# Turned blocks of a tile taken in the first two segments of the next tile, weight pieces in the others, and Q and K stored by one transfer

## The chip, the cores and the metric

The kernel runs on one core of one Trainium2 chip. The metric is the time of one execution on the device, in microseconds (us). One core has no second, slower state of a die to look out for: every run used here counts as fast, so all are compared with each other. "Ratio" always means the mean time of one kernel's fast runs over the mean of the other's fast runs of the same rounds, with a 95% interval, so it is not quite the ratio of the medians that stand beside it.

## The reference, cut to what matters

The reference computes the forward pass and all gradients of one layer: attention that runs over 64 segments in turn, each handing 8 memory rows to the next, then a gated feed-forward block. This is the recurrence that the change touches:

```python
mem = mem0                                    # 8 rows of 448
for s in range(n_seg):                        # 64 segments of 32 rows
    xs = x[:, s * seg_len:(s + 1) * seg_len, :]
    h = jnp.concatenate([mem, xs], axis=1)    # 40 rows
    q = jnp.einsum('btd,dhe->bhte', h, Wq)    # 16 heads of 256
    k = jnp.einsum('btd,dhe->bhte', h, Wk)
    v = jnp.einsum('btd,dhe->bhte', h, Wv)
    scores = jnp.einsum('bhqe,bhke->bhqk', q, k) * scale
    ...
    p = _softmax(scores, axis=-1)
    o = jnp.einsum('bhqk,bhke->bhqe', p, v)
    o = jnp.einsum('bhte,hed->btd', o, Wo)
    mem = o[:, :M, :]                         # the next segment waits for this
    outs.append(o[:, M:, :])
```

A segment cannot start before the previous one has given its memory rows, so the 64 segments are one chain. The backward pass needs Q, K, P and V of every segment, the attention output X_o with tokens on the partitions, and the weights turned. The kernel stores or turns all of these while the chain runs.

## The kernel before

The text of the kernel is the order in which work is emitted. A scheduler then places each instruction in its engine's list, by priority (the chain has the highest) and by when its own model expects the data to be ready. What is not tied to the chain can be moved far ahead of its place in the text. Each engine then works through its list.

Turning is done by DMA transposes that SP (SyncE) issues. They land in one of two staging buffers, and POOL (GpSimd) issues the save from there to DRAM:

```python
def stg():                      # the two staging buffers, dealt in turn
    rot[0] += 1
    for fn in unsaved.pop(rot[0] % 2, ()):
        fn()
    return stg_b[rot[0] % 2]

def save(*pairs):
    def fn():
        for out, in_ in pairs:
            nc.gpsimd.dma_start(out=out, in_=in_)              # L503
    unsaved[rot[0] % 2] = [fn]

def to_token_major(blk, t, ins=None):      # one tile (4 segments): two halves
    for hf in range(2):
        ot = stg()
        with tc.issue_after(ins) if ins is not None else nullcontext():
            nc.sync.dma_start_transpose(out=ot.rearrange(...), in_=blk[:, 16*hf:16*hf+16, :]...)   # L543
        save((dr["X_o"][t][:, hf * 2048:(hf + 1) * 2048], ot))

def piece():                               # one piece of a weight
    ...
    T, ot = dr["T" + nm], stg()
    ... nc.sync.dma_start_transpose(out=o3, in_=Ws[:, i0:i0 + n])          # L562, L563, L568
    save(...)
```

In the loop over segments (s is the segment, t the tile, r = s % 4, jm = s % 16), the attention of one segment, cut to its order:

```python
qk_rows(s, 0); qk_rows(s, 1)               # Q, K rows: L521, L525
qk_turned(s, 0)                            # turned on PE: L535
for w, nm in enumerate("qk"):              # L689: two stores, issued by ACT
    nc.scalar.dma_start(out=dr["T1" + nm][s], in_=qk_st[:, w]...)
value_rows(0)                              # V rows, K = 128: L633
pS0 = scores(0); softmax(0, pS0)           # mask L603, scores L609, Exp on ACT L618
qk_turned(s, 1); value_rows(1)
value_rest(0)                              # V rows, last 64 of K: four matmuls, L641;
                                           # both evacuations on ACT
pS1 = scores(1); p_in = softmax(1, pS1)
value_rows(2); transposed_p(0)             # P turned on PE: L652
value_rows(3); value_rest(2, p_in)
values(0); transposed_p(1); out_proj(0, 8) # L665, L678
values(1); out_proj(8, MC)
...
```

The end of a segment, where the staging buffers are dealt:

```python
nc.gpsimd.tensor_copy(out=mh[...], in_=hT_roll[...])       # POOL copies that the chain waits for
nc.gpsimd.tensor_copy(out=mblk[...], in_=orr)
...
if r == 1:
    ot = stg(); nc.sync.dma_start_transpose(...R_b...)     # T0
    save((dr["T0" + "qk"[w]][bm], ot))
if r < 3 and s >= 4:
    piece()
...
if r == 3:
    to_token_major(xblk, t, at)                            # both halves of this tile's block
if jm == 15:
    to_token_major(mblk, NT + s // 16, at)                 # the memory rows' block, then mh
    ...
```

POOL also copies the next segment's rest rows (L465, `rest_rows`), and fetches the rows of the residual back (L585).

Of the kernel before, what the change touches and what calls it, by code (L numbers as in the profile page):

```python
# [15 lines left out]
P = 128  # L16
# [129 lines left out]
def run_all(k: _K):  # L146
    nc, tc, ctx = k.nc, k.tc, k.ctx
    S, D, M, H, Dh, HD, F = k.S, k.D, k.M, k.H, k.Dh, k.HD, k.F
    SEG, L, NSEG, NT, KC, DP, MC, DC, FC = k.SEG, k.L, k.NSEG, k.NT, k.KC, k.DP, k.MC, k.DC, k.FC
# [54 lines left out]
    def dt(name, shape, dtype=BF16):  # L204
        return dram.tile(shape, dtype, name=name)
# [3 lines left out]
    dr = dict(XN=dt("XN", [NB * P, DP]), Hh=dt("Hh", [S, D]), HN=dt("HN", [S, D]), DH=dt("DH", [S, D], FP32),  # L209
              DHb=dt("DHb", [NB * P, DP]), Zt=dt("Zt", [S, F]), DGP=dt("DGP", [S, F]), DU=dt("DU", [S, F]),  # L210
              VG=dt("VG", [NSEG, 2 * L, W2]), XR=dt("XR", [NT * 32, DP]), P_all=dt("P_all", [NSEG, P, 8 * L]),
              X_o=dt("X_o", [NB, P, MC * P]), HC=dt("HC", [NB * P, DP]), Oh=dt("Oh", [S, D]))
# [2 lines left out]
        dr["M_" + nm] = dt("M_" + nm, [NT, P, MC * 32])  # L215
    for nm in ("q", "k", "v"):
        dr["T" + nm] = dt("T" + nm, [P, MC, D])
    for nm in ("q", "k"):
        dr["T1" + nm] = dt("T1" + nm, [NSEG, P, 1024])
        dr["T0" + nm] = dt("T0" + nm, [NSEG // 8, P, W2])  # L220
    dr["To"] = dt("To", [P, KC, HD])
    dr["Td"] = dt("Td", [P, KC, F])
# [14 lines left out]
def cj(j):  # L237
    return (j % 2) * 16 + j // 2
# [111 lines left out]
def forward_chain(k: _K):  # L350
    nc, tc = k.nc, k.tc
    S, D, M, H, Dh, HD = k.S, k.D, k.M, k.H, k.Dh, k.HD
    SEG, L, NSEG, NT, KC, DP, MC, DC = k.SEG, k.L, k.NSEG, k.NT, k.KC, k.DP, k.MC, k.DC
    X2 = k.aps["A_x"][0]
    MEM0 = k.aps["A_mem0"][0]
    ident, dr, sel, maskb = k.ident, k.dr, k.sel, k.maskb
# [11 lines left out]
    qk_st = A(15, 2, 2, 512)  # L368
# [3 lines left out]
    xblk_b = [A(52 - 24 * i, 32, P) for i in range(2)]  # L372
    mblk = A(44, 32, P)
# [108 lines left out]
    def prep_tile(t):  # L482
        if t >= NT:
            return
        nc.sync.dma_start_transpose(out=hx, in_=dr["XN"][t * P:(t + 1) * P, :])
        s0 = (4 * t) % NWIN
        for kc in range(KC):
            nc.gpsimd.tensor_copy(out=hT_roll[:, kc, s0:s0 + 4, 0:SEG], in_=hx[:, kc, :].rearrange("p (g j) -> p g j", g=4))
# [5 lines left out]
    def stg():  # L494
# [11 lines that stand above are left out]
    def save_all():  # L506
        for i in (1, 2):
            for fn in unsaved.pop((rot[0] + i) % 2, ()):
                fn()
# [21 lines left out]
    def qk_turned(s, b):  # L531
        pt = k.ps1()[:].bitcast(BF16)
        for w in range(2):
            for i in range(4):
                nc.tensor.transpose(pt[:, w * 512 + i * P:w * 512 + (i + 1) * P], qk_st[:, w, b, i * P:(i + 1) * P], ident[:, :])  # L535
        for w, dst in ((0, qT_b[s % 2]), (1, kT_b[s % 2])):
            k.evac(dst[:, 16 * b:16 * b + 16, M:L], pt[:, w * 512:(w + 1) * 512].rearrange("p (c n) -> p c n", n=32), "vs"[w])

    def to_token_major(blk, t, ins=None):
        for hf in range(2):  # L540
            ot = stg()
            with tc.issue_after(ins) if ins is not None else nullcontext():
                nc.sync.dma_start_transpose(out=ot.rearrange("p (a b) -> p a b", b=P),  # L543
                                            in_=blk[:, 16 * hf:16 * hf + 16, :].rearrange("p c n -> p (c n)"))
            save((dr["X_o"][t][:, hf * 2048:(hf + 1) * 2048], ot))

    pieces = []
    for nm, Ws in (("d", k.aps["B_w_down"]), ("o", k.Wo2)):
# [6 lines left out]
    def piece():  # L555
        if not pieces:
            return
        nm, Ws, i0, n = pieces.pop(0)
        T, ot = dr["T" + nm], stg()
        if nm in "do":  # L560
            o4 = ot.rearrange("p (c n) -> p c n", c=KC)
            nc.sync.dma_start_transpose(out=o4[:, 0:3, 0:n], in_=Ws[i0:i0 + n, 0:3 * P])  # L562
            nc.sync.dma_start_transpose(out=o4[:, 3, 0:n], in_=Ws[i0:i0 + n, D - P:D])  # L563
            save((T[:, 0:3, i0:i0 + n], o4[:, 0:3, 0:n]), (T[0:64, 3, i0:i0 + n], o4[64:P, 3, 0:n]))
        else:
            m = n // P
            o3 = ot[:, 0:m * D].rearrange("p (c d) -> p c d", d=D)
            nc.sync.dma_start_transpose(out=o3, in_=Ws[:, i0:i0 + n])  # L568
            save((T[:, i0 // P:i0 // P + m, :], o3))
# [18 lines left out]
    for s in range(NSEG):  # L588
        t, r = divmod(s, 4)
        jm = s % 16  # L590
# [3 lines left out]
        xblk, om2 = xblk_b[t % 2], om_b[s % 2]  # L594
        end = s == NSEG - 1
        if due and jm % 3 == 1:
            fetch(due[0], h_t, x2_t)
        with k.prio.crit():
# [29 lines left out]
            def value_rows(b):  # L628
                pV[b] = k.ps1()
                for kc in range(KC - 1):  # L630
                    for g in range(2):
                        n = 4 * g + b
                        nc.tensor.matmul(pV[b][64 * g:64 * g + 64, 0:512], lhsT=hT_flat[:, kc, sl * L:sl * L + 64],  # L633
                                         rhs=Wv_sb[:, kc, n * 512:(n + 1) * 512],
                                         start=(kc == 0), stop=False, skip_group_check=True)
# [49 lines left out]
                k.fl.at(0)  # L685
                k.fl.at(1)
            qk_turned(s, 0)
            for w, nm in enumerate("qk"):
                nc.scalar.dma_start(out=dr["T1" + nm][s], in_=qk_st[:, w].rearrange("p b n -> p (b n)"))  # L689
            value_rows(0)  # L690
            pS0 = scores(0)
            softmax(0, pS0)
# [23 lines left out]
            else:  # L716
# [3 lines left out]
                for e in range(2):  # L720
                    nc.tensor.transpose(pm[64 * e:64 * e + 64, 96:P], om2[32:64, P:P + 64], ident[32:64, 32:64])
                to_v = nc.vector.tensor_copy(  # L722
                    out=hT_roll[:, :, (s + 1) % NWIN, SEG:L].rearrange("p (d c) m -> p d c m", d=2),
                    in_=pm[:, 0:P].rearrange("p (c d m) -> p d c m", c=2, d=2)[:, :, :, 24:32])
# [15 lines left out]
        if due and jm % 3 == 0 and jm > 0:  # L740
            n = due.pop(0)
            residual(n, h_t, x2_t, to_v)
        save_all()
        if (r == 0 and t > 0) or s == 2:
            prep_tile(t + 2)
        if r == 1:
            w = bu // 4
            ot = stg()
            nc.sync.dma_start_transpose(out=ot.rearrange("p (a b) -> p a b", b=P), in_=R_b[bm % 2][w].rearrange("p c n -> p (c n)"))
            save((dr["T0" + "qk"[w]][bm], ot))  # L750
        if r < 3 and s >= 4:
            piece()
        at = None
        if jm == 15:
            px = k.fx1()
# [4 lines left out]
            due = list(range(t - 3, t + 1))  # L760
            if end:
                at = k.fl.at(3).ins
        if r == 3:
            to_token_major(xblk, t, at)
        if jm == 15:
            to_token_major(mblk, NT + s // 16, at)
            mrow = stg()
            nc.sync.dma_start_transpose(out=mrow[:, 0:DP].rearrange("p (a b) -> p a b", b=P),
                                        in_=mh.rearrange("p c n -> p (c n)"))
            r0 = (NT + s // 16) * P  # L770
            save((dr["XN"][r0:r0 + P, :], mrow[:, 0:DP]))
    save_all()
    assert not pieces and due == list(range(NT - 4, NT))
    late = [(B(0, D), B(0.875, D)), (W(61.5, D), W(62.375, D))]
# [178 lines left out]
def backward_chain(k: _K):  # L953
    nc, tc = k.nc, k.tc
    S, D, M, H, Dh, HD = k.S, k.D, k.M, k.H, k.Dh, k.HD
    SEG, L, NSEG, NT, KC, DP, MC, DC = k.SEG, k.L, k.NSEG, k.NT, k.KC, k.DP, k.MC, k.DC
    ident, dr, sel = k.ident, k.dr, k.sel
# [6 lines left out]
    WkT_sb, Q_sb = W(32, MC, D), W(60, 16, P)  # L964
    WvT_sb, K_sb = W(64, MC, D), W(92, 16, P)
# [23 lines left out]
    def load_v(s):  # L989
        return nc.sync.dma_start_transpose(out=vT, in_=dr["VG"][s])  # L990

    def load_seg(s):
        if s < NSEG - 1:
            load_v(s)
        for nm, T_sb in (("q", Q_sb), ("k", K_sb)):
            t1 = dr["T1" + nm][s].rearrange("(g x i) n -> g i x n", g=2, x=2)
            t0 = dr["T0" + nm][s // 8].rearrange("(x s i) (g n) -> s g i x n", x=2, s=8, g=2)
            for g in range(2):
                for src, i0, i1 in ((t1[g], M, L), (t0[s % 8, g], 0, M)):
                    nc.sync.dma_start(out=T_sb[64 * g + i0:64 * g + i1].rearrange("p (x c) n -> p x (c n)", x=2), in_=src)  # L1000
        P_sb = Pb[s % 2]
        nc.gpsimd.dma_start(out=P_sb.rearrange("p h n -> p (h n)"), in_=dr["P_all"][s])
        for g in range(2):
            pool_op = nc.gpsimd.tensor_copy(out=P_bd[64 * g:64 * g + L, :, g, :], in_=P_sb[64 * g:64 * g + L, :, :])
        stores("mid", s, pool_op.ins)
# [6 lines left out]
    def stores(place, seg, ins):  # L1012

        for fn in pending.pop((place, seg), []):
            with tc.issue_after(ins):
                fn()
# [34 lines left out]
    for s in range(NSEG - 1, -1, -1):  # L1051
        t, r = divmod(s, 4)
        jm = s % 16
# [3 lines left out]
        blk = {nm: blk_b[(3 * tb + i) % 5] for i, nm in enumerate("vkq")}  # L1057
# [3 lines left out]
        if s < NSEG - 1:  # L1061
            load_seg(s)

        with k.prio.crit():
            pss = [k.ps1() for _ in range(4)]
            for j in range(MC):
                c = cj(j)
                b, jj = divmod(j, 8)
# [96 lines left out]
        if r == 0:  # L1165
# [34 lines left out]
            t1 = k.f32("f3", D, "t1")  # L1200
# [224 lines left out]
```

## Time and profile before

| reading of before | value | where it is read |
|---|---|---|
| time, median of 3 | 3183.05 us (3175.76 to 3190.79) | the times |
| profiled run | 3198.43 us, span 3196.7 us | the page |
| PE busy | 2924.5 us, 91% | the page, part 1 |
| forward chain: start of segment 0 to start of segment 63 | 14.4 to 1057.6 us | timeline of PE, first matmul of L521 of each segment |
| steady segment | 15.09 us (14.75 in segments 56 to 62) | same |
| segments 17, 18, 20, 36, 52 | 21.2, 21.3, 22.3, 22.9, 21.6 us | same |

All segment durations below are read like that, from the first matmul of L521 in one segment to the first in the next.

Most of the span is a full PE, but a few segments last 6 to 7 us longer than their neighbours. The chain of waits, followed back from the end of the program, shows why. Its lines are: start, duration, what. This is before, in segment 36 (starts at 630.5 us):

```profile
626.94 0.08 PE po L678
627.02 6.96 DMA arA<-arA
...
634.54 0.54 POOL X_o L503
635.08 5.07 DMA arB<-Oh
...
640.60 0.63 DVE stats L580
```

PE leaves the chain at 627.02 us. A turned block (arA<-arA) takes 6.96 us to land; only then can POOL issue its save. The fetch of the residual's rows (arB<-Oh) stands behind the save in POOL's list and takes another 5.07 us; then DVE has work again, and its softmax comes behind that in its own list. None of this is arithmetic of the chain: the chain waits because POOL and DVE take their lists in order.

A second kind of stall is in segment 18 (338.3 to 359.6 us). This is the same view of before, there:

```profile
339.25 6.97 DMA arA<-in_A_Wo_dram
...
346.30 0.34 ACTq L689
346.69 0.59 ACT arA L76
```

ACT stands before the first of its two issues of L689 (K's store) until a turned weight piece of SP has landed: in the program the two share a semaphore. The evacuation that the chain needs comes only after it.

### The profile page before, as it was taken

The numbers are of one execution on the slowest core, as the hardware profiler recorded it, in microseconds if no ns is written. First come the engines' busy times: TensorE is split into PE (matmuls) and PEld (weight loads), VectorE is DVE, ScalarE is ACT, GpSimd is POOL, SyncE is SP. The second block draws the span as 40 slices with busy tenths as digits, with TensorE's granted clock in tenths as the row PEclk, the third lists the DMA queues.
The fourth block names the chain that finished last, engine by engine and source line by source line (L and its number), as shares of the span: only waits on it lengthen the run. The fifth ranks groups of instructions, "written<-read, shape, count | busy, mean of one in ns | idle before, by whom it ended". The sixth has DMA issues, their size and how long they took to land.

```text
span 3196.7 us, 107765 instructions
## 1 busy us (share of the span) xinstructions
PE 2924.5 (91%) x47442; PEld 1776.2 (56%) x47442; DVE 1364.9 (43%) x3433; ACT 1057.8 (33%) x2501; POOL 723.7 (23%) x1648
## 2 busy tenths in 40 slices
PE   6899899989988869977999999999999699999998
PEld 3455455555544547645666666666666454444444
DVE  4455455455455567753444544445444201111110
ACT  2444344344434323322333333333433101110210
POOL 2232332223232221121112211112211111111111
PEclk9999999999999979988999999999999899999999
DMA  6968765867667888894454555445545898959952
GB/s 237 198 152 177 181 163 141 194 162 183 167 155 192 246 207 195 191 274 147 132 138 137 132 149 134 140 132 140 144 134 141 266 269 226 198 181 195 191 147 72
DMA packets 757305, 556.21 MB, mean 174 GB/s; under 512 B 627732, under 2 KB 656388, under 8 KB 754404
## 3 DMA queue, kind: packets, MB, share of 16 engines
q1 hardware_dynamic: 671828, 294.81, 44.2%
q0 software_dynamic: 66576, 220.95, 20.3%
q10 hardware_dynamic: 18432, 33.56, 3.1%
q8 instruction: 372, 6.09, 0.8%
q14 instruction: 97, 0.79, 0.1%
HBM read 167.32 MB, written 234.23 MB: 126 GB/s over the span
## 4 chain that ended last, share of the span: by engine, by line
PE 69%; DMA 10%; DVE 9%; issue 7%; ACT 3%; SPq 2%; POOL 1%; ACTq 0%; POOLq 0%; DVEq 0%
PE psf L1286 8%; PE po L1120 7%; PE psf L1071 7%; PE psf L633 5%; PE psf L521 4%; PE psf L1048 4%; PE psf L1307 4%; PE po L678 3%; PE fx L1184 3%; PE psf L847 2%; DVE arA L75 2%; PE fx L454 2%; PE fx L937 2%; PE fx L1291 2%; PE psf L1142 2%
## 5 line engine op out<-in xcount | busy, mean ns | idle before, releaser
L75 DVE CAST arA<-psf 128x256 bf16<-128x256 f32 (+4 forms) x997 | 470.8, 492 | 920.1 <-PE psf L1286 258.9
L76 ACT CAST arA<-psf 128x384 bf16<-128x384 f32 (+6 forms) x979 | 390.0, 420 | 1179.8 <-PE psf L1286 256.5
L1120 PE MATMUL po<-arW,arA 128*32 128x448 bf16 x6144 | 348.9, 357 | 22.8 <-DVE arA L75 20.5
L633 PE MATMUL psf<-arW,arA 128*64 128x512 bf16 x1536 | 253.3, 393 | 0.0
L1286 PE MATMUL psf<-arW,arA 128*128 128x512 bf16 x1000 | 252.0, 379 | 0.0
L1071 PEld LDWEIGHTS <-arW 128*128 128x128 bf16 x8192 | 214.1, 96 | 27.5 <-issue 27.5
L1120 PEld LDWEIGHTS <-arA 128*32 128x32 bf16 x6144 | 152.1, 97 | 135.9 <-DVE arA L75 21.7
L1286 PEld LDWEIGHTS <-arA 128*128 128x128 bf16 x1440 | 136.0, 98 | 164.8 <-issue 13.8
L1071 PE MATMUL psf<-arA,arW 128*128 128x40 bf16 x8192 | 217.7, 180 | 8.4 <-DVE arA L1146 5.1
L521 PE MATMUL psf<-arW,arA 128*32 128x512 bf16 x3072 | 193.9, 385 | 12.5 <-DVE arA L722 12.5
L847 PE MATMUL psf<-arW 128*128 128x256 bf16 x1344 | 159.3, 281 | 45.1 <-DMA arW<-arW 34.3
L847 PEld LDWEIGHTS <-arW 128*128 128x128 bf16 x1344 | 134.9, 101 | 71.5 <-DMA arW<-arW 29.1
L678 PE MATMUL po<-arW,arA 128*32 128x256 bf16 (+1 forms) x4096 | 142.4, 265 | 9.8 <-DVE arA L75 6.8
L1048 PEld LDWEIGHTS <-arW 128*128 128x128 bf16 x2048 | 87.6, 100 | 89.6 <-issue 62.9
L1048 PE MATMUL psf<-arB,arW 128*128 128x80 bf16 x2048 | 98.1, 202 | 41.4 <-DMA arW<-T0k 22.6
L454 PE MATMUL fx<-arA,arW 128*128 128x64 bf16 (+1 forms) x2048 | 84.8, 196 | 43.2 <-ACT arB L76 30.7
L1081 ACT COPY arA<-psf 128x1024 bf16<-128x1024 bf16 x128 | 123.3, 1015 | 2.3 <-PE psf L1080 0.4
L521 PEld LDWEIGHTS <-arA 128*32 128x32 bf16 x3072 | 70.5, 96 | 90.1 <-DVE arA L722 18.1
L76 ACT COPY arA<-psf 128x512 bf16<-128x512 bf16 (+2 forms) x136 | 79.0, 582 | 111.5 <-DVE arA L75 87.9
L678 PEld LDWEIGHTS <-arA 128*32 128x32 bf16 x4096 | 94.6, 97 | 30.2 <-DVE arA L75 10.2
L633 PEld LDWEIGHTS <-arA 128*64 128x64 bf16 x1536 | 85.0, 111 | 44.1 <-issue 1.4
L454 PEld LDWEIGHTS <-arW 128*128 128x128 bf16 (+1 forms) x2048 | 71.2, 99 | 65.4 <-issue 43.8
(285 smaller groups left out, 4618.6 us busy)
## 6 DMA issues: line engine op xcount, KB each, us to landing
X_o<-arA POOLq DMA_DIRECT2D x40, 512.0 KB, 4.1
T1k<-arA ACTq DMA_DIRECT2D x64, 256.0 KB
T1q<-arA ACTq DMA_DIRECT2D x64, 256.0 KB
arW<-T1q SPq DMA_DIRECT2D x128, 128.0 KB
arW<-T1k SPq DMA_DIRECT2D x128, 128.0 KB
X_v<-arA POOLq DMA_DIRECT2D x32, 512.0 KB, 5.3
X_k<-arA POOLq DMA_DIRECT2D x32, 512.0 KB, 3.8
X_q<-arA POOLq DMA_DIRECT2D x32, 512.0 KB, 3.6
```

What stands on the lines that cost most here:

```text
L75: return nc.vector.tensor_copy(out=out, in_=in_)
L76: return nc.scalar.copy(out=out, in_=in_)
L454: nc.tensor.matmul(banks[w][:, i * 64:(i + 1) * 64], lhsT=lhsT, rhs=xr[lo:hi, kc, :], start=(kc == 0 and i == 0), stop=(kc == KC - 1), ski ...
L521: nc.tensor.matmul(banks[w][32 * q:32 * q + 32, :], lhsT=hT_roll[:, kc, sl, M:L], rhs=(Wq_sb, Wk_sb)[w][:, kc, col(q, b)], start=(kc == 0) ...
L633: nc.tensor.matmul(pV[b][64 * g:64 * g + 64, 0:512], lhsT=hT_flat[:, kc, sl * L:sl * L + 64], rhs=Wv_sb[:, kc, n * 512:(n + 1) * 512], sta ...
L678: nc.tensor.matmul(pO[32 * q:32 * q + 32, 0:w], lhsT=xblk[:, j, r * SEG:(r + 1) * SEG], rhs=Wo_sb[:, cj(j), 256 * dh:256 * dh + w], start= ...
L847: nc.tensor.matmul(ps[:, f2 * 256:(f2 + 1) * 256], lhsT=Wt[:, kc, c * P:(c + 1) * P], rhs=xT[:, kc, :], start=(kc == 0), stop=(kc == KC - 1))
L1048: nc.tensor.matmul(ps[b][:, i * 2 * L:(i + 1) * 2 * L], lhsT=lhs[:, at, :], rhs=rhs_bd[:, cl // 2, :, :].rearrange("p g n -> p (g n)"), st ...
L1071: nc.tensor.matmul(pss[b][:, jj * L:(jj + 1) * L], lhsT=WoT_sb[:, kc, c * P:(c + 1) * P], rhs=do_roll[:, kc, sl, :], start=(kc == 0), stop ...
L1120: nc.tensor.matmul(pH[32 * (j % 4):32 * (j % 4) + 32, 0:D], lhsT=blk[nm][:, j, r * SEG:(r + 1) * SEG], rhs=WT[:, cj(j), :], start=(nm == " ...
L1286: nc.tensor.matmul(pa[2 * kc + g][:, 0:w], lhsT=lhs_of(b)[:, kc * P:(kc + 1) * P], rhs=rhs_of(b, g), start=(b == 0), stop=(b == nblk - 1), ...
L1307: nc.tensor.matmul(pa[i][:, 0:D], lhsT=lhs_of(b, i), rhs=rhs_of(b), start=(bi == 0), stop=(bi == len(nblk) - 1))
```

## The change

The intent is threefold. Turned blocks wait for their tile, so put them into the first two segments of the next tile, one half each; then no segment has two of them, and behind a sixteenth segment (jm = 15) three turnings stand in place of five. Weight pieces wait for nothing, so let them fill the other places. And store Q and K by one transfer of 512 KB in place of two of 256 KB, which saves ACT one issue per segment. The title of the change also says "behind the first exponential"; the text puts the store ahead of the first value rows, and leaves its place on ACT to the scheduler.

```diff
+    dr["T1"] = dt("T1", [NSEG, P, 2, 1024])
     for nm in ("q", "k"):
-        dr["T1" + nm] = dt("T1" + nm, [NSEG, P, 1024])
...
-    def to_token_major(blk, t, ins=None):
-        for hf in range(2):
-            ot = stg()
...
+    def to_token_major(blk, t, hf, ins=None):
+        ot = stg()
...
             qk_turned(s, 0)
-            for w, nm in enumerate("qk"):
-                nc.scalar.dma_start(out=dr["T1" + nm][s], in_=qk_st[:, w].rearrange("p b n -> p (b n)"))
+            nc.scalar.dma_start(out=dr["T1"][s], in_=qk_st.rearrange("p w b n -> p w (b n)"))
...
-        if r == 1:
+        if s >= 4 and ((r > 0 and jm < 15) or (jm == 0)):
+            piece()
+        if r == 2:
             w = bu // 4
             ot = stg()
             nc.sync.dma_start_transpose(out=..., in_=R_b[bm % 2][w]...)
             save((dr["T0" + "qk"[w]][bm], ot))
-        if r < 3 and s >= 4:
-            piece()
...
-        if r == 3:
-            to_token_major(xblk, t, at)
         if jm == 15:
-            to_token_major(mblk, NT + s // 16, at)
+            for hf in range(2):
+                to_token_major(mblk, NT + s // 16, hf, at)
...
+        if t > 0 and r < 2:
+            to_token_major(xblk_b[(t - 1) % 2], t - 1, r)
+        if end:
+            for hf in range(2):
+                to_token_major(xblk, t, hf, at)
...
-        for nm, T_sb in (("q", Q_sb), ("k", K_sb)):
-            t1 = dr["T1" + nm][s].rearrange(...)
+        for w, (nm, T_sb) in enumerate((("q", Q_sb), ("k", K_sb))):
+            t1 = dr["T1"][s, :, w].rearrange(...)
```

In the order in which a tile takes the two staging buffers A and B (H is half a turned block, p a weight piece), before is `p T0 p p H H`, and after is `H p H p T0 p`. As the buffers alternate, before puts pieces into both buffers, so that a piece waits for the block ahead of it in its buffer. After puts pieces into one buffer alone; only behind a sixteenth segment do three other turnings (two halves of the memory rows' block, then mh) take from both.

More of the change, by code (lines that the diff above doesn't have):

```diff
@@ L537, in qk_turned @@
             k.evac(dst[:, 16 * b:16 * b + 16, M:L], pt[:, w * 512:(w + 1) * 512].rearrange("p (c n) -> p c n", n=32), "vs"[w])
-    def to_token_major(blk, t, ins=None):
-        for hf in range(2):
-            ot = stg()
-            with tc.issue_after(ins) if ins is not None else nullcontext():
-                nc.sync.dma_start_transpose(out=ot.rearrange("p (a b) -> p a b", b=P),
-                                            in_=blk[:, 16 * hf:16 * hf + 16, :].rearrange("p c n -> p (c n)"))
-            save((dr["X_o"][t][:, hf * 2048:(hf + 1) * 2048], ot))
+    def to_token_major(blk, t, hf, ins=None):
+        ot = stg()
+        with tc.issue_after(ins) if ins is not None else nullcontext():
+            nc.sync.dma_start_transpose(out=ot.rearrange("p (a b) -> p a b", b=P),
+                                        in_=blk[:, 16 * hf:16 * hf + 16, :].rearrange("p c n -> p (c n)"))
+        save((dr["X_o"][t][:, hf * 2048:(hf + 1) * 2048], ot))
     pieces = []
@@ L994, in load_seg @@
             load_v(s)
-        for nm, T_sb in (("q", Q_sb), ("k", K_sb)):
-            t1 = dr["T1" + nm][s].rearrange("(g x i) n -> g i x n", g=2, x=2)
+        for w, (nm, T_sb) in enumerate((("q", Q_sb), ("k", K_sb))):
+            t1 = dr["T1"][s, :, w].rearrange("(g x i) n -> g i x n", g=2, x=2)
             t0 = dr["T0" + nm][s // 8].rearrange("(x s i) (g n) -> s g i x n", x=2, s=8, g=2)
```

## The prediction

> **What bounds it.** The change touches the forward chain (64 segments, 14 to 1076 us); backward reads the same bytes of Q and K. In the timeline of PE a steady segment takes 15.09 us, PE nearly full. Above that, stalls stand in a few segments (starts of L521): segments 4 and 5 about 9 us, 16 to 20 about 17, 32 to 36 about 9, 48 to 52 about 8: some 43 us. The chain of waits shows their cause: turning transfer on SP (L543, L562, L568), its save on POOL (L503), the next turning that needs the staging buffer; behind them POOL's copies and row fetches, and an ACT store (L689) that waits until an SP transfer on its semaphore has landed.
>
> **Intent.** Three turnings behind a sixteenth segment in place of five, and one ACT issue (0.33 us) fewer per segment. If every stall went, the gain were 43 us, 1.3%: over 2% faster is nearly impossible.
>
> **What moves instead** (order listings of both kernels):
> 1. Two staging buffers are taken in turn. After the change two are taken in most segments, so one gets weight pieces only, the other turned blocks and T0. The piece buffer then depends on nothing in the chain, and the scheduler hoists pieces: on SP eight stand at segments 3 to 6, twelve each at about 15 to 20, 31 to 36, 47 to 52, none between. Before, blocks that waited for their segment held them to three per four segments.
> 2. Their saves are hoisted into POOL's queue too, among the copies that the chain needs (L465 rest rows, the first 8 rows, the residual's fetches). POOL takes instructions in order (the Trainium skill, TensorE: Matmul & The Clock Gate, Part 2, says that PE alone reorders; the trace agrees: from 300 us on POOL idles 110 us at L503 for turned blocks). A piece takes about 6.5 us from issue to landing, its save 4.4: a buffer turns round in 11 us, twelve need 130 us where five to six segments give 75 to 90. POOL stands still, then DVE (it may not overwrite rows that POOL has not copied), then PE.
> 3. PE's order changes: scores of the first four heads move behind the second value rows; ACT does two evacuations (0.53 us each) before the first Exp, and both Exps follow together. P transposes and values come later.
>
> **Costing.** I laid both listed orders out with the trace's durations and landing medians (an estimate). Before comes out at 15.21 us a steady segment, with stalls in the right segments, though 30 us too little in sum. After: steady 15.46 (+0.25, some 15 us in all, on the critical path), about 30 us at segments 6 to 8 and 25 to 35 us at each of the three groups, longest at segments 19, 35 and 51 (35 to 40 us each). In sum +127 us; with landings 15% shorter +69, 25% shorter +36, 15% longer +180. I take +125. The five turnings before the feed-forward phase are reordered: within 5 us.
>
> **Predicted:** 3308 us, 3230 to 3395. Faster by over 2%: 0.03; within 2%: 0.13; slower: 0.84.
>
> **What would show it.** Segments 19, 35, 51 over 25 us, steady ones 15.3 to 15.5. POOL idle before L503 for weight pieces at least three times that of before; DVE waiting for POOL; no L567 on SP in segments 24 to 30 and 38 to 46; ACT idle longer before the first Exp. Time after the forward chain unchanged within 10 us.
>
> **What would make it wrong.** Landings much shorter when transfers run one at a time (then +30). POOL's copies having more slack than I gave them. If the burst costs nothing, 3160 to 3200 us.

## More of the kernel before

Segments 16 to 18, 32 to 34 and 48 to 50 carry extra PE work (16.45 us without a stall).

The costliest line of POOL's idle time in front of its saves, by what ended it (us, times), from before's instructions of L503 between 60 and 1070 us:

```profile
  DMA arA<-arA: 121.3, 35
```

## The result, and the profile after

| | before | after |
|---|---|---|
| time, median of 4 | 3186.92 us (3175.76 to 3193.65) | 3282.67 us (3265.64 to 3288.62) |
| ratio of fast runs | 1 | 1.0295 (1.0244 to 1.0347) |
| profiled run: time, span | 3198.43, 3196.7 us | 3265.64, 3263.8 us |
| PE busy between segments 0 and 63 (after 75 us) | 894 us | 938 us |
| start of segment 63 | 1057.6 us | 1129.2 us |
| from there to the end | 2139.0 us | 2134.7 us |
| steady segment; 56 to 62; 16 | 15.09; 14.75; 16.45 us | 15.45; 15.45; 18.05 us |
| longest segments | 36: 22.9, 20: 22.3, 5: 21.8 us | 19: 36.5, 35: 32.4, 51: 27.1, 8: 25.5 us |

The result is correct and 3% slower, and the whole loss of the profiled runs lies in the forward chain: start of segment 63 is 71.6 us later, and what follows is 4.3 us shorter. These two executions differ by 67.2 us and the medians by 95.8: before's profiled execution is slower than any of its four timed ones, after's is the fastest of its four. The account by segments below is of this pair; where the other executions lose the remaining 29 us, no trace shows.

The chain of waits of after in segment 19 (370.2 to 406.7 us), lines as above:

```profile
387.46 4.02 DMA arA<-in_B_w_gate_dram
...
392.02 2.75 DMA Tg<-arA
394.80 4.08 DMA arA<-in_B_w_gate_dram
...
399.41 2.78 DMA Tg<-arA
402.20 3.23 DMA arA<-in_B_w_gate_dram
...
405.97 0.55 POOL Tg L503
406.52 2.42 DMA arB<-Oh
```

From 379.35 us on (one more round stands ahead of these lines), the chain of the whole program runs through one staging buffer for 27 us: a weight piece is turned into it, then saved, and then the next is turned. A round takes 7.3 to 8.1 us (379.35 to 387.46 to 394.80 to 402.20). On SP, pieces from segment 16 on stand only in bursts, and each burst begins behind the turning of mh (L765) of a sixteenth segment: the scheduler did not move pieces ahead of that. At the end, as in before, POOL gets past its save and issues the fetch, and DVE follows.

What the chain does not show is why the attention waits for weight pieces that only the backward pass uses. PE stops twice in this segment, and the timelines show two paths (start, duration, engine, line, operation, out<-in, count, idle before and what ended it). The timeline of POOL, for the same segment of after:

```profile
383.84 0.57 POOL L503 DMA_DIRECT2D Tg<-arA  x1 [5.52 <-DMA arA<-in_B_w_gate_dram]
392.02 0.55 POOL L503 DMA_DIRECT2D Tg<-arA  x1 [7.62 <-DMA arA<-in_B_w_gate_dram]
392.57 0.99 POOL L465 COPY arA<-arW 128x128 bf16<-128x128 bf16 x4
...
399.41 0.54 POOL L503 DMA_DIRECT2D Tg<-arA  x1 [5.35 <-DMA arA<-in_B_w_gate_dram]
399.95 0.75 POOL L737 COPY arA<-arB 128x256 bf16<-128x256 bf16 x2
```

POOL stands idle for 7.62 us in front of one save, and the copies of the rest rows (L465) that the next segment's scores read are next in its list. Behind the save after that stand the copies of L737, and on these hangs the second stop of PE (timelines of DVE and PE):

```profile
400.39 0.23 DVE L75 CAST arB<-psf 128x64 bf16<-128x64 f32 x1 [9.34 <-POOL arA L737]
400.96 0.69 PE L664 MATMUL psf<-arB,arW 128*128 128x80 bf16 x8 [9.24 <-ACT arB L76]
```

DVE and ACT may not write new rows of `orr` before POOL has copied the old ones. The first stop does not end in POOL's list (timelines of ACT and PE):

```profile
383.39 0.33 ACTq L687 DMA_DIRECT2D T<-arA  x1
383.76 1.07 ACT L76 COPY arA<-psf 128x512 bf16<-128x512 bf16 x2 [9.28 <-DMA arA<-in_B_w_gate_dram]
384.49 0.46 PE L608 MATMUL psf<-arA 128*40 128x40 bf16 x16 [7.65 <-ACT arA L76]
```

Here ACT waits at the issue of its store until a weight piece has landed that uses the same semaphore, as in before's segment 18, and the evacuation of the turned K and Q is behind it. Of PE's stops of over 0.8 us in segments 6 to 54, 37 us end in a copy of POOL (segments 8, 19, 35 and 51, the last two with 15.09 and 9.36 us) and 19 us in ACT's store behind a turning (segments 6, 7, 8, 19, 21 and 37).

The Trainium skill, "DMA: Bandwidth & Descriptors", section "Issuing engines are not separate DMA queues", says that issuing from several engines saves only the sequencer's time, usually small beside the transfer. No run here tests that for bandwidth. Here the price is another: an issue that waits on another engine's transfer also stops everything behind it on its own engine.

The same line for L503 in after, between 60 and 1140 us:

```profile
  DMA arA<-arA: 194.4, 39
```

Turned blocks made POOL idle for 121.3 us before, and for 194.4 us now. Summed over the lines for weight pieces (in_A and in_B sources) it went from 158 to 177 us only, in 29 waits before and 39 after: no longer ones (5.5 us in the mean before, 4.5 after), but bunched in the bursts.

A long stall costs a little more than its wait. The view of stretches gives, for after's segments 19 and 41, duration and PE busy first, and the granted clock in the third number from the end:

```profile
370.20:406.70 36.50, 18.96 (x286) 10.67 (x285) 8.32 (x25) 7.24 (x18) 9.23 (x22) 0.67 0.60 158
762.65:778.10 15.45, 14.65 (x278) 8.27 (x278) 7.94 (x25) 6.79 (x17) 4.89 (x13) 1.00 0.61 180
```

and for before's segments 19 and 40:

```profile
359.50:375.50 16.00, 15.96 (x288) 8.96 (x284) 7.94 (x23) 6.56 (x16) 3.71 (x12) 1.00 0.36 82
698.72:713.81 15.09, 14.03 (x279) 7.96 (x279) 7.90 (x24) 6.76 (x17) 2.77 (x9) 1.00 1.09 217
```

In segment 19 about as many matmuls took 18.96 us of PE in place of 15.96, at a mean clock of 0.67. (one_store, below, which has after's lists and no stall here, needs 14.65 us of PE for its segment 19.) The Trainium skill, "TensorE: Matmul & The Clock Gate", Part 1, "What's actually happening", says that PE falls to half its clock after an idle window of about 3.4 us and needs as long a busy one to recover. The clock in this trace agrees with the half and with the length of the window: it is 0.50 from 378.99 to 389.23 us and from 392.64 to 406.30 us, three and four times 3.41 us. It does not agree with a whole idle window: the clock fell 2.15 and 0.91 us after PE had stopped. In the steady segments both kernels have the full clock, so the 15.45 against 15.09 us is not the clock's.

It is the lists'. PE in before's segment 40, cut to scores (L609), groups of four value matmuls (L641), turned P (L652) and values (L665):

```profile
704.16 0.54 PE L609 MATMUL psf<-arA 128*40 128x40 bf16 x14
...
705.29 0.41 PE L641 MATMUL psf<-arW,arA 64*64 64x512 bf16 x4
...
706.91 0.27 PE L652 MATMUL fx<-ident,arB 128*40 128x40 bf16 x8
...
707.78 0.41 PE L641 MATMUL psf<-arW,arA 64*64 64x512 bf16 x4
708.12 0.46 PE L665 MATMUL psf<-arB,arA 128*128 128x80 bf16 x8
```

and in after's segment 41 (lines moved by one; it starts at 762.65 us, before's at 698.72):

```profile
768.87 0.40 PE L640 MATMUL psf<-arW,arA 64*64 64x512 bf16 x2
769.20 0.38 PE L608 MATMUL psf<-arA 128*40 128x40 bf16 x16
769.50 0.40 PE L640 MATMUL psf<-arW,arA 64*64 64x512 bf16 x2
...
771.62 0.41 PE L640 MATMUL psf<-arW,arA 64*64 64x512 bf16 x3
772.31 0.27 PE L651 MATMUL fx<-ident,arB 128*40 128x40 bf16 x8 [0.27 <-DVE arB L622]
772.51 0.40 PE L640 MATMUL psf<-arW,arA 64*64 64x512 bf16 x1
...
773.17 0.46 PE L664 MATMUL psf<-arB,arW 128*128 128x80 bf16 x8
```

The scores come 5.4 us after the segment's start in before, 6.6 us in after; the first values 9.4 and 10.5 us. And four value matmuls take 0.41 us together but 0.40 us for two and 0.40 us for one: they fill the four quarters of the array at once. (The Trainium skill, "TensorE: Matmul & The Clock Gate", Part 3, "Measured speedup vs the span model", gives a group of matmuls on different tiles of the array the time of one and about 4 ns for each further one; 0.41 us for four and 0.40 for one agree.) So each split group costs a pass: PE busy is 14.65 in place of 14.03 us.

ACT in these two segments, before:

```profile
705.52 0.34 ACT L618 ACTIVATE S_sb<-S_sb 128x160 f32<-128x160 f32 x1 [0.21 <-DVE S_sb L617]
705.76 1.06 ACT L76 CAST arA<-psf 128x512 bf16<-128x512 f32 x2
```

and after:

```profile
769.94 1.07 ACT L76 CAST arW<-psf 128x512 bf16<-128x512 f32 x2 [0.69 <-PE psf L640]
770.90 0.61 ACT L617 ACTIVATE S_sb<-S_sb 128x160 f32<-128x160 f32 x2
```

Before, the first Exp comes 6.8 us after the segment's start and the two evacuations of value rows follow; after, the evacuations stand first, and the Exp comes at 8.25 us.

Now the sum. Between segments 6 and 63, before spends 874.0 us if its stalled segments are given the length of their unstalled likes, and 34.6 us more in stalls. After spends 980.4 us. The run with the single store alone (one_store, below) spends 905.2 us with hardly a stall, which sets the price of the lists; what after has above it, segment by segment, is the price of its own stalls:

| us, segments 6 to 63 | before | after |
|---|---|---|
| before's lists, no stall | 874.0 | 874.0 |
| the other lists (905.2 - 874.0) | | +31.2 |
| stalls of before | +34.6 | |
| stalls of after: segments 6 to 8, 16 to 21, 32 to 37, 48 to 54 | | +12.7, +22.6, +21.6, +18.3 |
| sum | 908.6 | 980.4 |

### The profile page after: what moved, and what is told of

It is laid out like the page before. It is cut to its first block, busy times and chain, and to the rows that moved or that the text cites. A ratio compares the mean times of both kernels' runs of the same rounds, so it can differ in the third digit from the quotient of the medians.

```text
span 3263.8 us, 107654 instructions
## 1 busy us (share of the span) xinstructions
PE 2968.1 (91%) x47432; PEld 1795.5 (55%) x47442; DVE 1367.6 (42%) x3433; ACT 1060.7 (32%) x2501; POOL 725.0 (22%) x1648
## 4 chain that ended last, share of the span: by engine, by line
PE 62%; DMA 14%; DVE 11%; issue 8%; ACT 3%; POOL 1%; SPq 1%; POOLq 0%; ACTq 0%; DVEq 0%
PE psf L1288 8%; PE po L1122 7%; PE psf L1073 6%; PE psf L521 4%; PE psf L1050 4%; PE psf L1309 4%; PE po L677 3%; DVE arA L75 3%; PE fx L1186 3%; PE psf L849 2%; PE psf L632 2%; PE fx L939 2%; DMA arA<-arA 2%; PE fx L1293 2%; PE psf L1144 2%
## 5 line engine op out<-in xcount | busy, mean ns | idle before, releaser
L632 PE MATMUL psf<-arW,arA 128*64 128x512 bf16 x1536 | 205.0, 389 | 2.6 <-ACT arA L76 2.6
L76 ACT CAST arB<-psf 128x96 bf16<-128x96 f32 (+1 forms) x320 | 84.0, 262 | 65.3 <-POOL arA L737 33.7
L632 PEld LDWEIGHTS <-arA 128*64 128x64 bf16 x1536 | 71.5, 110 | 57.3 <-issue 5.9
L640 PE MATMUL psf<-arW,arA 64*64 64x512 bf16 x512 | 102.8, 405 | 0.0
```

The costliest lines, as they stand in the source:

```text
L76: return nc.scalar.copy(out=out, in_=in_)
L632: nc.tensor.matmul(pV[b][64 * g:64 * g + 64, 0:512], lhsT=hT_flat[:, kc, sl * L:sl * L + 64], rhs=Wv_sb[:, kc, n * 512:(n + 1) * 512], sta ...
```

## The experiments

Two theories were to be told apart first. Mine: the loss comes from the new places, through one chain: pieces have a staging buffer of their own, so the scheduler moves them forward into bursts, and their saves stop POOL. The rivals: that the single store does it through the lists, or that the places cost something other than the bursts (a buffer shared otherwise, blocks that come later). Twelve kernels ran.

| run | kernel | median us | ratio to before (95%) | start of segment 63 |
|---|---|---|---|---|
| one_store | before + single store | 3200.73 | 1.0057 (1.0027 to 1.0086) | 1057.6 |
| places_only | after with two stores | 3287.71 | 1.0327 (1.0301 to 1.0353) | 1160.4 |
| block_first | after, block dealt before the piece | 3203.14 | 1.0052 (1.0037 to 1.0068) | 1054.8 |
| held | after, pieces held to their segment | 3200.56 | 1.0043 (1.0029 to 1.0058) | 1053.3 |
| free_saves | after, saves wait for no piece (wrong result) | 3260.13 | 1.0224 (1.0209 to 1.0239) | 1114.9 |
| behind_exp | before + single store behind the Exp | 3164.53 | 0.9929 (0.9910 to 0.9948) | 1034.2 |
| behind_held | behind_exp + held pieces | 3156.99 | 0.9914 (0.9892 to 0.9936) | 1031.1 |
| block_first_behind | block_first + store behind the Exp | 3165.24 | 0.9938 (0.9912 to 0.9963) | 1042.0 |
| second_whole | one_store, second value group whole | 3228.7 | 1.0128 (1.0103 to 1.0153) | 1085.1 |
| both_whole | one_store, both groups whole | 3186.76 | 0.9984 (0.9961 to 1.0007) | 1046.2 |
| after_whole | after, both groups whole | 3280.7 | 1.0287 (1.0257 to 1.0317) | 1143.5 |
| exp_ahead | one_store, Exp ahead of the evacuations | 3204.01 | 1.0053 (1.0023 to 1.0084) | 1070.5 |

All but free_saves are correct. The profiled executions of behind_held and block_first_behind are their slowest (3175.73 and 3190.71 us), so the last column is too high for these two.

### Halves of the change: one_store and places_only

one_store is before with the three hunks of T1 alone (`dr["T1"]`, the single `dma_start`, the load of the backward pass). places_only is after with these three undone.

> Before with only the single Q and K store; turnings placed as before. Listing: PE, ACT and DVE orders are those of the changed kernel (scores behind the second value rows), SP's order nearly that of before, no burst of pieces. Theory (order and bursts are two separate costs): steady segments 15.45 us, segments 56 to 62 15.45, 16 to 18 about 18, no segment from 18 on over 22 us; some 35 us lost by order, 10 to 25 of before's 43 us of stalls gained back, so 3190 to 3215 us. Rival A (only the bursts cost; PE's order is hidden): steady 15.1 and at most 3187 us. Rival B (the one large store is the whole cost): 3270 to 3290 us.

Measured: steady segments 15.45, segments 16 to 18 18.05, 18.05, 17.51 us, as in after, and no segment from 6 on above 18.1 us. So the single store alone makes the other lists, and it also removes before's stalls: they cancel within 4 us in the chain (908.6 and 905.2 us from segment 6 on), and the time rises by 0.6%.

> The changed kernel with two stores as before. Listing: PE, ACT and DVE orders of before, bursts of pieces on SP as in the changed kernel. Theory: steady segments 15.09 us, stalls of over 25 us at segment 19 or 20, 35 or 36, 51 or 52, as large as in the changed kernel or larger, since the shorter segments give the burst less time: 3215 to 3260 us. Rival A (bursts are the whole cost): 3270 us or more. Rival B (the store is the whole cost): 3185 us or less.

Measured: 3287.71 us, above my range and where the rival stood. The bursts are there with before's PE list (steady 15.09 us), and the stalls are larger than after's: segment 20 lasts 43.6, 36 45.3, 52 41.7 us, and all stalls from segment 6 on come to 137 us, against after's 75. So the places alone bring the loss, and the two costs do not add. That after's slower segments give the bursts more time to finish is a part of it at most: if the chain lost only what does not fit beside a fixed amount of transfers, the segments of a burst would take equally long in both, but segments 6 to 8, 16 to 21, 32 to 37 and 48 to 54 take 59.1, 122.7, 121.7 and 133.9 us in after and 64.3, 137.8, 134.7 and 147.0 us in places_only. What makes the rest was not taken apart.

### Two ways of undoing the bursts: block_first and held

block_first changes one place in after, so that blocks and pieces again alternate over both buffers:

```diff
             prep_tile(t + 2)
+        if t > 0 and r < 2:
+            to_token_major(xblk_b[(t - 1) % 2], t - 1, r)
         if s >= 4 and ((r > 0 and jm < 15) or (jm == 0)):
             piece()
...
-        if t > 0 and r < 2:
-            to_token_major(xblk_b[(t - 1) % 2], t - 1, r)
```

> The changed kernel with two lines exchanged: in each segment the turned block takes its staging buffer before the weight piece does. The same transfers in the same segments, but then each of the two buffers holds a block of every tile, and the listing shows two to three pieces per tile, no bursts. Theory (hoisted pieces, freed by a buffer of their own, block POOL): no segment from 18 on over 24 us, steady still 15.45, 3195 to 3225 us. Rival C (blocks put off into the next tile, or more turnings per segment, cost by themselves through the DMA engines): stalls stay at 19, 35 and 51 and the time stays within 15 us of 3283.

Measured: 3203.14 us. No segment from 6 on is above 19 us, and steady segments keep 15.45 us.

held leaves the dealing as it is in after, one buffer for pieces alone, but orders each piece's turning on SP behind the V store of its own segment:

```diff
-    def piece():
+    def piece(ins):
...
-            nc.sync.dma_start_transpose(out=o3, in_=Ws[:, i0:i0 + n])
+            with tc.issue_after(ins):
+                nc.sync.dma_start_transpose(out=o3, in_=Ws[:, i0:i0 + n])
...
-            piece()
+            piece(vg.ins)          # vg: the V store of this segment
```

> The changed kernel, with every weight piece's turning queued on SP behind the V store of its own segment. Which buffer a piece takes stays as changed (pieces have one to themselves); only the hoisting is forbidden, and the listing shows one piece per segment. Theory (the hoisting is what costs): no segment from 18 on over 22 us, steady 15.45, 3195 to 3225 us, as block_first. Rival E (the dealing of the buffers itself costs, since blocks and T0 now share one): stalls at 19, 35 and 51 stay over 25 us and the time over 3250.

Measured: 3200.56 us, no such stall at all. held and block_first differ in the buffers and have in common only that no piece runs ahead; both take away the whole burst. So it is the running ahead that costs, not the buffer of its own and not the blocks that come a tile later.

### Is POOL the place? free_saves

The saves of the pieces write a resident weight in place of the turned piece, so that POOL need not wait for the turning (the result is wrong):

```diff
-            save((T[:, i0 // P:i0 // P + m, :], o3))
+            save((T[:, i0 // P:i0 // P + m, :], Wv_sb[:, 0, 0:m * D].rearrange("p (c d) -> p c d", d=D)))
```

> The changed kernel; the saves of the weight pieces write a resident weight tile in place of the turned piece, so POOL need not wait for a piece to land. Wrong on purpose: the turned weights, so most gradients, are false; sizes and number of transfers are the same. The pieces are hoisted on SP as before or more. Theory (POOL standing still in front of a piece's save is most of the burst's cost; SP's own waits in order are the rest): segments 19, 35 and 51 under 24 us, 3205 to 3260 us. If POOL is all of it: 3190 to 3205. Rival F (the burst costs through SP or the DMA engines, not through POOL): over 3270 us.

Measured: segments 19, 35 and 51 fall from 36.5, 32.4 and 27.1 to 16.3, 15.7 and 15.6 us. The bursts are still on SP in segments 16 to 20, 32 to 36 and 48 to 51, but from segment 6 on the chain takes 923.2 us, against 980.4 in after and 905.2 in one_store: 57 of the 75 us of stalls are gone. So the round of turning and save is the path of the three long stalls. The run does not part the two ends of it: without the round, POOL no longer waits for pieces, and ACT's store also waits less (1.81 us in place of 8.83 in segment 19). That POOL is the larger one is read from after's trace above; after with its store held behind the Exp, which would part them, was not run.

The time fell by 22 us only, because the start got worse: segments 4 and 5 last 34.6 and 46.9 us. Freed of their saves, the pieces run ahead still further, and now SP is what is held in order, as the chain of waits of free_saves shows there:

```profile
147.87 7.98 SPq L561
155.85 0.05 issue
155.94 11.56 SPq L562
```

ACT's store in segment 5 waits 29 us there, until a V store of SP that stands behind these issues has landed. Take one in-order list away, and the same burst stands in the next one.

### The single store as it was meant: behind_exp, behind_held, block_first_behind

The scheduler had put the store on ACT ahead of the evacuations of the turned Q and K. Here it is tied behind the first Exp (in before, so without the new places):

```diff
-            nc.scalar.dma_start(out=dr["T1"][s], in_=qk_st.rearrange("p w b n -> p w (b n)"))
             value_rows(0)
             pS0 = scores(0)
             softmax(0, pS0)
+            with tc.issue_after(e_in[0].ins):      # e_in[0]: the first Exp
+                nc.scalar.dma_start(out=dr["T1"][s], in_=qk_st.rearrange("p w b n -> p w (b n)"))
```

> Before with the single store held behind the first Exp on ACT, which the change meant and did not get. Listing: scores of the first heads come right after their turning, ahead of the second value rows; no bursts. Theory: with the Exp ahead of store and evacuations the steady segment is 15.0 to 15.15 us, and an ACT store that waits for an SP transfer no longer holds the first Exp: stalls of before halved, 3150 to 3180 us. Rival D (a single store costs wherever it stands): steady 15.4 and 3190 us or more.

Measured: 3164.53 us, 0.7% faster than before, with steady segments of 14.92 us. The timeline of ACT in a segment of behind_exp that starts at 698.41 us:

```profile
705.07 0.34 ACT L620 ACTIVATE S_sb<-S_sb 128x160 f32<-128x160 f32 x1
705.14 0.33 ACTq L694 DMA_DIRECT2D T<-arA  x1
705.59 1.07 ACT L76 CAST arW<-psf 128x512 bf16<-128x512 f32 x2 [0.19 <-ACT S_sb L620]
```

The Exp is at 6.7 us in the segment, the evacuations behind it. The same single transfer is worth +0.6% or -0.7%, by its place and by the lists that the scheduler makes around that place.

behind_held adds held's ordering of the pieces to this.

> Turnings placed as before, pieces held to their segments, single store held behind the first Exp: candidate for a version that beats both. Theory: steady 14.92 us, what is left of stalls in behind_exp (segments 17, 38, 40) goes, since SP has at most one piece per segment: 3145 to 3165 us. If the pieces' places do not matter once the store is behind the Exp: 3160 to 3170.

Measured: 3156.99 us, the lowest median of all; its interval overlaps that of behind_exp, so the further 0.15% is not certain.

block_first_behind takes the intent of the change in full: new places without bursts, store behind the Exp.

> The whole intent of the change, mended: blocks in the next tile, turned block ahead of the piece in its segment, single store held behind the first Exp. Theory: steady 14.92 us, no burst, at the sixteenth segment three turnings in place of five: 3145 to 3170 us. If putting the blocks off into the next tile brings nothing by itself: the same as behind_exp, 3160 to 3170.

Measured: 3165.24 us, the same as behind_exp, which has before's places. So the deferral of the blocks into the next tile brings nothing that these intervals show, once the single store has taken before's stalls away.

### What in the other lists costs 0.36 us a segment? second_whole, both_whole, exp_ahead

Theory A was that PE's split groups of value matmuls are the price (0.34 us for each further part), rival B that it is ACT's late Exp. second_whole is one_store with one move in the text:

```diff
             value_rows(2)
-            transposed_p(0)
             value_rows(3)
             value_rest(2, p_in)
+            transposed_p(0)
```

> The kernel before with the single store, and the transposes of the first four heads' P written after the last four value matmuls in the program, so that PE's list has these four 64x512 matmuls in one group (v4, then P) in place of three, P, one. The first such group stays split two and two around the scores, and ACT's order is that of one_store (two evacuations ahead of the first Exp). Theory A (the price of the order is PE's: four matmuls of 64 rows and 64 columns run at once in the array's four quarters and take 0.34 us as a group, but split they take 0.34 us for each part): one of two splits is gone, so steady segments fall from 15.45 to 15.1-15.2 us, and segments 16 to 18 fall by 0.2 to 0.4 too. Time 3175 to 3195. Rival B (the price is ACT's, the late Exp): steady segments stay at 15.4-15.5, time 3195 to 3210.

Measured: 3228.7 us, above both forecasts; steady segments last 15.95 us, longer by half a microsecond, although PE's busy time fell (14.65 to 14.51 us). With P turned later, PE now waits before P, before its second part and before the values. Theory A in this form is wrong.

both_whole also puts the first group behind the first scores:

```diff
+                        with tc.issue_after(sc_in[b0 // 2].ins):   # last matmul of scores(b0 // 2)
                             nc.tensor.matmul(pV[b0 + e][...], ...)
```

> As second_whole, and the first group of four held behind the first scores too, so neither is split; one evacuation of value rows still stands ahead of the first Exp on ACT, and the store stays where the scheduler put it, ahead of the exponentials. Theory A: steady segments 14.85 to 15.1 us, so at least as short as before's 15.09, and time 3160 to 3180, near that of behind_exp without moving the store. Rival B: 15.3 or more, time above 3190.

Measured: steady segments 15.47 us. PE's busy time is 14.00 us, so the two extra passes are gone, but the segment is no shorter. In a segment that starts at 684.23 us, PE waits before the second part of P, right after the whole group and the first part:

```profile
694.16 0.25 PE L655 MATMUL fx<-ident,arB 128*40 128x40 bf16 x4 [0.79 <-ACT arB L76]
```

What was won on PE is lost waiting for ACT's evacuation of the turned P, which stands behind a value evacuation. The time is that of before (0.9984), because segments 18, 34 and 50 fell by 2 us each and before's stalls stay gone.

exp_ahead is the opposite corner: PE's groups stay split, but ACT's two evacuations are held behind the first Exp.

```diff
-                    with tc.issue_after(held.ins) if held is not None and e == 1 else nullcontext():
+                    with tc.issue_after(held.ins) if held is not None and e == 1 else tc.issue_after(e_in[0].ins) if held is None else nullcontext():
```

> The kernel before with the single store left where the scheduler puts it, and the two evacuations of the first value rows held on ACT behind the first Exp. PE's list keeps both groups of four value matmuls split (two and two around the scores, two and two around P), so it is the corner that both_whole is not: there the groups were whole and one evacuation still stood ahead of the Exp, and nothing was won. If the price of the order is ACT's (the Exp, and the evacuation of the transposed P, come late), steady segments fall from 15.45 to 15.2 or less, time 3165 to 3185. If it takes both (late Exp and split groups each are enough to cost it), they stay at 15.4 or more, time 3190 or more. Segments 16 and 32 (18.05) fall below 17.8 in the first case.

Measured: 3204.01 us, steady segments 15.88 us; the case "it takes both". The Exp comes earlier (7.7 us in the segment), PE is as busy as with split groups (14.60 us), and PE stands still for 0.68 us behind the second part of P, until an evacuation of ACT. So neither PE's groups nor ACT's order alone is the price of the lists. behind_exp, in which scores stand right behind the turned K, groups are whole, and the Exp is first, is the only one that has the gain. Which further piece of its order is needed was not taken apart.

### Do the two costs add? after_whole

The changed kernel with both_whole's edits.

> The changed kernel, placement untouched, with both groups of four kept whole as in both_whole. Theory: steady segments near those of both_whole (14.85 to 15.1), some 25 us less over the chain if the stalls stayed as they are; but the bursts of weight pieces then have less time to finish, as in places_only, so the stalls at 8, 19 or 20, 35 or 36 and 51 or 52 grow and eat most of it: time 3260 to 3290. If the two costs simply added: about 3245 to 3255.

Measured: 3280.7 us, as good as after's 3282.67. Its steady segments did not shorten (15.47 us), so the test is weaker than I meant it. But segments 17, 18, 33, 34, 49 and 50 have less to do, and the stalls above both_whole came to 89 us, against 75 in after: again less work beside the bursts went with longer stalls.

## Why the prediction was right or wrong, point by point

The predicted time, 3308 us, was 25 us above the measured 3282.67, within the range, and "slower" was right.

- **"one gets weight pieces only ... the scheduler hoists pieces": right.** held and block_first show it by taking it away, and places_only by having it without the store. The trace shows no L567 on SP in segments 24 to 30, as predicted, and a single one (at 718.3 us, early in segment 38) in segments 38 to 46.
- **"POOL stands still, then DVE ..., then PE": right for the larger part.** 37 us of PE's stops end in a copy of POOL, and free_saves removes the three long stalls. But 19 us end in ACT's store, which waits for a turning on its semaphore. The prediction had this path for before's stalls and left it out of the burst's.
- **"Segments 19, 35, 51 over 25 us, steady ones 15.3 to 15.5": right** (36.5, 32.4, 27.1; 15.45 us). The first Exp came later, and ACT waited longer in front of what stands ahead of it (0.69 against 0.21 us).
- **"a buffer turns round in 11 us": too long.** The round took 7.3 to 8.1 us. I had added two medians of before (6.5 us for a piece, 4.4 us for its save). They were taken where several transfers run together, which is the likely reason but was not tested. The same four pieces of w_gate can be compared: their turning landed after 5.2 us in before and 4.0 in after, their save after 4.9 us and 2.8 (medians). The prediction named this itself as what could make it wrong (landings "much shorter when transfers run one at a time").
- **"about 30 us at segments 6 to 8 and 25 to 35 us at each of the three groups": too large, by that term.** It was 12.7, 22.6, 21.6 and 18.3 us, 75 in place of 105 to 135.
- **"+0.25, some 15 us in all": too small.** The lists cost 31 us: 13.4 us in the plain segments 6 to 55, a third of a us each, 12.8 us in the nine segments with extra PE work (1.1 to 1.6 us each), and 5.0 us in segments 56 to 62 (0.71 us each). The plain ones had been laid out well (15.46 predicted, 15.45 measured); the other two were missed: they were 18 us of the 31.
- **"POOL idle before L503 for weight pieces at least three times that of before": wrong.** It was 158 and 177 us. The idle time in front of turned blocks grew (121 to 194 us). In before, too, POOL waited for pieces, 6.49 and 7.85 us in segments 25 and 29 for example, which last 15.09 us like the others. What matters is what stands behind the wait in the list, not its sum.
- **"Time after the forward chain unchanged within 10 us": right** (2139.0 and 2134.7 us).

The stall term was too large by some 30 to 60 us and the list term too small by 16 us, so the two errors partly cancelled. A third error: the layout of before had 30 us of stalls too few, as the prediction said, and nothing was taken off for it; the measured loss is net of the 34.6 us of stalls that after no longer has. The loss of the profiled pair is 67 us, so a forecast of 125 is 58 us too high for the executions that the trace explains; that it lies only 25 us above the measured median is in part luck. The experiments add what the prediction did not have: the two terms are not independent. Of the runs with bursts, those with shorter segments had longer stalls (75 us in after, 89 in after_whole, 137 in places_only).

The intent did not fail for lack of a gain to be had. The gain in stalls (34.6 us) was real, but one_store shows that the single store brings it by itself. The title's "behind the first exponential" did not come about: the scheduler put the store ahead of the evacuations. Tied there, it was the only part of the change that paid.

Left open: which part of behind_exp's lists, beyond whole groups and an early Exp, makes its 14.92 us; and why its segments 3 and 4 (23.1 and 21.3 us) stall.

## What to carry to other kernels

Work that depends on nothing is not free filler where a scheduler deals it out: a dependency, even an accidental one through a shared buffer, may be what spreads it, and a burst of it can block every in-order engine that issues its transfers or shares a semaphore with them. Tie such work to a place by an explicit order, and tie a store that is meant to be behind something to that thing. When a change touches an engine's list, lay out also the segments that carry extra work, and time a transfer from places where it runs as it will run after the change.

## What the Trainium skill lacked or had wrong

- "DMA: Bandwidth & Descriptors", "Issuing engines are not separate DMA queues", gives the sequencer's time as all that issuing from several engines saves. It does not say what an issue that waits for another engine's transfer costs the work behind it: POOL stood 7.62 us in front of one save, and the three longest stalls (36.5, 32.4, 27.1 us segments) went when these waits were taken away (16.3, 15.7, 15.6 us).
- The same page, "Latency and other measured facts", gives a fixed cost of about 2 us and an effective rate for transposing transfers, but no landing time of one instruction. Here the turning of a 512-column piece of w_gate landed after 5.2 us (median of four) in before, and after 4.0 in after, where pieces ran one at a time; its save after 4.9 and 2.8 us.
- "TensorE: Matmul & The Clock Gate", Part 3, describes what overlaps when matmuls on different tiles follow each other. It has no number for the reverse, a group that other work splits, which pays a pass for each part: 0.41 us for four 64x512 matmuls together, 0.40 us for two and 0.40 us for one.
